# Linear attention woven into an MLP: the second batch's attention rewoven, its neighbour's exps moved ahead, own PSUM banks for one chunk

## The chip, the cores and the metric

The kernel runs on one core of one Trainium2 chip. The metric is the device time of one execution in microseconds (us). All runs quoted gave the reference's result.

## The reference, cut to what matters

```python
def _attn_ref(q, k, v):                 # q, k, v: (8 batches, 8 heads, 576, 64)
    q_s = exp(q - max);  q_s = q_s / sum over the last axis
    k_s = exp(k - max);  k_s = k_s / sum over the sequence
    kv = np.einsum('bhsd,bhse->bhde', k_s, v)
    return np.einsum('bhsd,bhde->bhse', q_s, kv)

def _moe_ref(x, w_in, w_out, beta):     # x: (4608, 512)
    h = x @ w_in                        # (4608, 2048)
    g = h * (1.0 / (1.0 + np.exp(-beta * h)))
    return g @ w_out                    # (4608, 512)
```

## The kernel before: the parts that matter

The rows are handled in nine chunks of 512. Chunk n takes batch n's first 512 rows, one chunk the eight remainders. For each chunk TensorE does 64 products for `h` (16 tiles, four products each) and 64 for the output, `acc`; the scalar engine does a tanh per h tile and VectorE makes `g` from it. The attention of the next batch is woven between those products: exp of q, its sums and division, transposes of q; exp of k, a cast of v, the `kv` products; then `x = kv` times `q`, and casts of x into `xT`.

There are eight PSUM banks (H0 to H2, A0, A1, X0, X1, K), and each h tile is given one by name. A bank can be written again only when its last reader is done; for an h tile the last reader is the VectorE instruction that makes `g`. `LAG = 4` keeps the output products four h tiles behind.

```python
    def h_bank(n, i):
        ...                                   # chunk 0 has its own list
        if n == 1 and i < 7:
            return ("A0", "H0", "H2", "H1", "A1", "K", "X0")[i]
        return f"H{(n * NJ + i + 1) % 3}"
```

Batches 0 and 1 are done early and by hand. Batch 0 is the head of the kernel; batch 1 stands between the output products of chunk 0 (`b_mm(m)` emits m of them) and the first h tiles of chunk 1 (`unit_mm(1, i, k0, k1)`). `eq_exp, eq_sum, eq_div, eq_t` treat q, `ek_exp` k, `ev_cast` v; `ekv_mm` is the kv product with a column of ones that gives the sums, and `eks_mm` computes the sums alone, ahead of it.

```python
    def batch_1():
        b_mm(32)
        eq_exp(1, 0)
        eq_exp(1, 1)
        eq_sum(1, 0)
        eq_div(1, 0, nc.gpsimd)
        b_mm(16)
        ...                                   # k exps, eq_sum(1, 1), eq_div(1, 1, nc.gpsimd), v casts
        b_mm(12)
        eq_t(1, 0, "X0", nc.vector)
        ekv_open(1, 0, ("X1", "K"))
        ekv_mm(1, 0)
        ...                                   # normalise, k exps of half 1, eq_t(1, 1)
        b_mm(2)
        x_group(1, (0,), ["X0", "H1"])
        ...
        b_mm(2)
        ekv_open(1, 1, ("X1", "K"))
        eks_mm(1, 1)
        ...                                   # v casts; unit_mm(1, 0..4, 0, 1)
        ekv_mm(1, 1)
        ...
        x_group(1, (1,), ["X0", "X1"])
        ...
        for m in range(2):
            q_exp(2, m)                       # two of batch 2's four; the others between tanhs
        ...
```

The head, cut to the lines that matter:

```python
    ev_cast(0, 0, 1, nc.gpsimd)               # GpSimd casts the second part of v's first half
    eq_t(0, 0, "X0", nc.scalar)
    dummy(1)                                  # a product that only keeps TensorE at work
    ekv_open(0, 0, ("X1", "K"))
    ekv_mm(0, 0)                              # needs that cast
    ...
    eks_mm(0, 1)
    bt = bank("A1", [P, 4, 4], F32, "bt")
    for i in range(4):
        nc.tensor.transpose(bt[:, i], beta_r[:, i:CH:4], identf[:])
    x_group(0, (0,), ["X0", "A0"])
```

The softmax here doesn't subtract the row's maximum and nothing guards it: scores larger than these inputs give would overflow.

## Time and profile before

| | before |
|---|---|
| time, median of three runs | 287.14 us (286.94 to 287.20) |
| time of the execution that was profiled | 286.0 us, at a mean granted clock of 1.000 |
| span of the profile | 284.3 us |
| first output product of chunk 0 starts | 29.70 us |
| fifth h tile of chunk 1 done | 52.78 us |
| first h product of chunk 2 | 69.40 us |
| products of h and acc | 0.2163 us each, one after another |

The profile's last 215 us are an unbroken row of products, so everything that this change could move lies before 70 us.

### The profile page before, as it was taken

To read this page: it belongs to the slowest core of one execution; us is meant where nothing else is said; L and a number is where in the kernel's file an instruction comes from. 1 tells how busy PE (TensorE), PEld (TensorE's weight loads), DVE (VectorE), ACT (ScalarE), POOL (GpSimd) and SP (SyncE) were. 2 spreads that over 40 slices of the span, in tenths; PEclk is the share of its full clock that TensorE was granted. 3 is DMA by queue.
4 is the path that set the end of the run, shared out by engine and by line. 5 is a ranking of instruction groups with operands and counts; after the bars stand their busy time and mean duration, and the time that the engine had idled before them with its cause. 6 is when DMAs were issued, how large, how long until landed. Compare 5 with 4: busy or idle time off the path is not lost.

```text
span 284.3 us, 4675 instructions
## 1 busy us (share of the span) xinstructions
PE 275.3 (97%) x1708; PEld 136.0 (48%) x1708; DVE 154.7 (54%) x283; ACT 168.2 (59%) x280; POOL 73.1 (26%) x120
## 2 busy tenths in 40 slices
PE   7599999999999999999999999999999999999995
PEld 3455445344454445444444444444444444444444
DVE  2858356886856385647664665467553333344401
ACT  4656374985974578557854785568453544454411
POOL 3378851360451045103610261017000000000000
PEclk9999999999999999999999999999999999999999
DMA  7999999749879916990699149903310200031112
GB/s 234 378 391 408 386 384 357 273 83 362 223 159 323 243 72 141 335 284 0 147 285 324 43 111 292 322 35 90 98 37 2 75 37 37 2 75 37 38 75 74
DMA packets 51559, 51.69 MB, mean 182 GB/s; under 512 B 21068, under 2 KB 41932, under 8 KB 51536
## 3 DMA queue, kind: packets, MB, share of 16 engines
q1 hardware_dynamic: 51360, 51.33, 59.8%
q8 instruction: 13, 0.21, 0.3%
q14 instruction: 10, 0.08, 0.1%
q10 hardware_dynamic: 144, 0.07, 0.1%
q0 software_dynamic: 32, 0.01, 0.0%
HBM read 38.28 MB, written 9.44 MB: 168 GB/s over the span
## 4 chain that ended last, share of the span: by engine, by line
PE 91%; ACT 3%; DMA 3%; DVE 1%; SPq 1%; issue 0%; ACTq 0%
PE acc L511 44%; PE h L459 43%; DMA v<-in_v_dram 3%; PE x L410 2%; PE kv L386 2%; ACT Ek L230 1%; DVE g L473 1%; ACT xT L152 1%; ACT th L471 0%; ACT kvn L281 0%; PE kv L258 0%; SPq L117 0%; ACT qT L152 0%; PE xt L424 0%; DVE qT L166 0%
## 5 line engine op out<-in xcount | busy, mean ns | idle before, releaser
L473 DVE SCALAR_TENSOR_TENSOR g<-th,h 128x512 bf16<-128x512 bf16 x144 | 97.4, 685 | 97.4 <-ACT th L471 97.1
L471 ACT ACTIVATE th<-h,beta_h 128x512 bf16<-128x512 f32 x144 | 97.2, 687 | 84.5 <-PE h L459 82.5
L511 PE MATMUL acc<-w_out_b,g 128*128 128x512 bf16 (+2 forms) x608 | 145.5, 368 | 0.5 <-DVE g L473 0.4
L459 PE MATMUL h<-xT,w_in_b 128*128 128x512 bf16 x512 | 129.1, 379 | 0.6 <-ACT xT L152 0.6
L459 PEld LDWEIGHTS <-w_in_b 128*128 128x128 bf16 x576 | 64.9, 113 | 61.4 <-issue 1.4
L511 PEld LDWEIGHTS <-g 128*128 128x128 bf16 x608 | 56.9, 98 | 65.5 <-issue 3.2
L317 POOL TENSOR_TENSOR Eq<-Eq,qz 128x512 bf16<-128x512 bf16 x24 | 25.1, 1049 | 87.2 <-issue 41.0
L540 ACT ACTIVATE o<-acc 128x512 f32<-128x512 f32 x34 | 20.1, 592 | 10.0 <-PE acc L511 10.0
L161 POOL TENSOR_SCALAR_AFFINE_SELECT va<-v 128x256 bf16<-128x256 f32 (+2 forms) x53 | 20.3, 420 | 8.2 <-DMA v<-in_v_dram 7.9
L357 ACT ACTIVATE Ek<-k 128x640 bf16<-128x640 f32 x24 | 17.5, 729 | 0.0
L315 DVE TENSOR_REDUCE qz<-Eq 128x8 f32<-128x512 bf16 x24 | 16.2, 677 | 0.5 <-ACT Eq L307 0.5
L459 PE MATMUL h<-xTt,w_in_b 128*128 128x512 bf16 x64 | 16.4, 379 | 0.0
L307 ACT ACTIVATE Eq<-q 128x512 bf16<-128x512 f32 x24 | 14.9, 624 | 0.0
L166 DVE CAST xT<-x 128x512 bf16<-128x512 f32 x16 | 10.9, 684 | 0.8 <-PE x L410 0.8
L152 ACT CAST xT<-x 128x512 bf16<-128x512 f32 x16 | 9.3, 579 | 2.2 <-PE x L410 2.2
L161 POOL TENSOR_SCALAR_AFFINE_SELECT w_in_b<-wi 128x512 bf16<-128x512 f32 x16 | 9.5, 612 | 3.0 <-DMA wi<-in_moe_w_in_dram 2.8
L201 DVE TENSOR_REDUCE qz<-Eq 128x16 f32<-128x1024 bf16 x4 | 4.9, 1218 | 9.8 <-ACT Eq L194 9.8
L343 POOL TENSOR_TENSOR Et<-Et,zt 128x512 bf16<-128x512 bf16 x4 | 4.2, 1042 | 21.0 <-DVE zt L342 21.0
L194 ACT ACTIVATE Eq<-q 128x1024 bf16<-128x1024 f32 x4 | 4.2, 1056 | 8.4 <-DMA q<-in_q_dram 8.4
L161 POOL TENSOR_SCALAR_AFFINE_SELECT w_out_b<-wo 128x1024 bf16<-128x1024 f32 x8 | 8.3, 1039 | 1.9 <-DMA wo<-in_moe_w_out_dram 1.8
L584 PE MATMUL warm<-zf 128*128 128x512 f32 (+2 forms) x12 | 7.1, 731 | 1.5 <-DVE zf L551 1.5
L529 DVE TENSOR_SCALAR o<-acc 128x256 f32<-128x256 f32 (+1 forms) x2 | 0.7, 358 | 9.7 <-PE acc L511 9.7
(53 smaller groups left out, 86.8 us busy)
## 6 DMA issues: line engine op xcount, KB each, us to landing
q<-in_q_dram SPq DMA_DIRECT2D x16, 512.0 KB, 5.6
out_dram<-o SPq DMA_DIRECT2D x31, 256.0 KB, 4.2
k<-in_k_dram SPq DMA_DIRECT2D x24, 320.0 KB, 7.1
v<-in_v_dram SPq DMA_DIRECT2D x24, 320.0 KB, 7.5
wo<-in_moe_w_out_dram SPq DMA_DIRECT2D x8, 512.0 KB, 11.0
wi<-in_moe_w_in_dram SPq DMA_DIRECT2D x6, 512.0 KB, 8.2
k<-in_k_dram SPq DMA_DIRECT2D x4, 576.0 KB, 9.0
v<-in_v_dram SPq DMA_DIRECT2D x6, 288.0 KB, 8.6
```

What stands on the lines that cost most here:

```text
L152: nc.scalar.copy(dst, src)
L161: nc.gpsimd.affine_select(out=dst, in_=src, pattern=[[0, n]], base=0, channel_multiplier=0, compare_op=ALU.is_equal, fill=fill0,)
L166: eng.tensor_copy(dst, src)
L307: nc.scalar.activation(by_pair(Eq[b], m).rearrange("p t h d -> p h t d"), ld["q", b, hf][:, a : a + 2, :].rearrange("p h (t d) -> p h t d" ...
L315: nc.vector.tensor_reduce(z, e, axis=AX.X, op=ALU.add)
L317: nc.gpsimd.tensor_tensor(e, e, z.unsqueeze(3).to_broadcast((P, NT, 2, D)), ALU.mult)
L357: nc.scalar.activation(Ek[b][:, :, h0:h1, :].rearrange("p t h d -> p h t d"), ld["k", b, hf][:, a : a + h1 - h0, :].rearrange("p h (t d) - ...
L459: nc.tensor.matmul(hs[n, i][:], w_in_b[:, kt, blk * CH + r : (blk + 1) * CH : 4], rhs_a(n, kt), start=(kt == 0), stop=(kt == KT - 1),)
L471: nc.scalar.activation(th[:], h[:], ACTF.Tanh, scale=beta_h[:, i // 4, i % 4 : i % 4 + 1])
L473: nc.vector.scalar_tensor_tensor(out=g[:], in0=th[:], scalar=1.0, in1=h[:], op0=ALU.add, op1=ALU.mult)
L511: nc.tensor.matmul(acc[n, st][:, c0:c1], gs[n, j][:, min(st, 3) * P : (min(st, 3) + 1) * P], w_out_b[:, j, c0:c1], start=(j == 0), stop=(j ...
L540: nc.scalar.activation(o[:], acc[n, st][:], ACTF.Copy, scale=0.5)
```

## The change

The intent is to take the small waits of TensorE out of batch 1 and chunk 1. The core of the diff:

```diff
     def h_bank(n, i):
-        if n == 1 and i < 7:
-            return ("A0", "H0", "H2", "H1", "A1", "K", "X0")[i]
-        return f"H{(n * NJ + i + 1) % 3}"
+        if n == 1:
+            return ("A0 X1 K X0 A1 H0 H2 H1 X1 H0 H2 H1 H0 H2 H0 H1").split()[i]
+        return f"H{(n * NJ + i) % 3}"
 ... b_mm: one h tile more of lag for chunk 1, j < 4
 ... head:
+    bt = bank("A1", [P, 4, 4], F32, "bt")     # the four beta transposes, before the first of q
 ...
-    dummy(1)
+    dummy(1, 2 * P)
 ...
-    ev_cast(0, 1, 1, nc.scalar, 0, 3)
-    ev_cast(0, 1, 1, nc.vector, 3, 6)
-    ev_cast(0, 1, 1, nc.gpsimd, 6, KT9)
+    ev_cast(0, 1, 1, nc.vector, 0, 5)
+    ev_cast(0, 1, 1, nc.gpsimd, 5, KT9)
     ekv_rk(0, 1)
+    ekv_mm(0, 1)                              # was after the casts of w_in
 ... batch_1:
-        eq_div(1, 0, nc.gpsimd)
-        b_mm(16)
+        eq_div(1, 0, nc.vector)
         for c in range(2):
             ek_exp(1, 0, c)
+        b_mm(20)
         eq_sum(1, 1)
 ...                                           # eq_div(1, 1, nc.vector), k exps earlier
+        b_mm(3)
+        ekv_open(1, 0, ("H0", "H1"))
         ekv_mm(1, 0)
+        b_mm(1)
+        eq_t(1, 1, "H2", None)
 ...
-        eks_mm(1, 1)                          # the pass for the sums alone is gone
 ...
+        b_mm(4)
+        x_group(1, (0,), ["X0", "H0"])
+        ekv_open(1, 1, ("X1", "K"))
+        ekv_mm(1, 1)
 ...
+        b_mm(4)
 ...
+        x_group(1, (1,), ["H1", "H2"])
 ...
-        for m in range(2):
+        for m in range(4):
             q_exp(2, m)                       # batch 2's exps of q, all ahead of chunk 1's tanhs
 ...
-        for m in range(2):
+        for m in range(3):
             q_norm(2, m)
 ... chunks 1 and on:
-            for g in range(2):                # batch 2's x, two groups of four products
-                at(n, 12 + 2 * g, ... x_group(b, (g,), ["X0", "X1"]))
-            at(n, 10, ... x_group(b, (0, 1), ["X0", "X1", "A0", "K"]))
+        at(n, s + 10, ... x_group(b, (0, 1), ["H1" if n == 1 else "A0", "X0", "X1", "K"]))
```

More of the change, by code (lines that the diff above doesn't have):

```diff
@@ L502, in b_mm @@
             n, st, j = bq[pos[0]]
-            if n * NJ + j + LAG > done_a[0] and done_a[0] < NCH * NJ - 1 and n:
+            if n * NJ + j + LAG + (n == 1 and j < 4) > done_a[0] and done_a[0] < NCH * NJ - 1 and n:
                 break
@@ L595 @@
     eq_div(0, 1, nc.vector)
-    nc.vector.tensor_reduce(even[:], evens[:], axis=AX.X, op=ALU.add)
     ev_cast(0, 0, 1, nc.gpsimd)
+    bt = bank("A1", [P, 4, 4], F32, "bt")
+    for i in range(4):
+        nc.tensor.transpose(bt[:, i], beta_r[:, i:CH:4], identf[:])
     eq_t(0, 0, "X0", nc.scalar)
-    dummy(1)
+    dummy(1, 2 * P)
     ekv_open(0, 0, ("X1", "K"))
@@ L607 @@
     ekv_norm(0, 0, nc.vector, nc.scalar)
+    nc.vector.tensor_scalar(
+        beta_h[:], bt[:].rearrange("p i b -> p b i"), 0.5, None, op0=ALU.mult
+    )
+    nc.vector.tensor_reduce(even[:], evens[:], axis=AX.X, op=ALU.add)
     ekv_open(0, 1, ("X1", "K"))
     eks_mm(0, 1)
-    bt = bank("A1", [P, 4, 4], F32, "bt")
-    for i in range(4):
-        nc.tensor.transpose(bt[:, i], beta_r[:, i:CH:4], identf[:])
     x_group(0, (0,), ["X0", "A0"])
     ev_cast(0, 1, 0, nc.gpsimd)
-    ev_cast(0, 1, 1, nc.scalar, 0, 3)
-    ev_cast(0, 1, 1, nc.vector, 3, 6)
-    ev_cast(0, 1, 1, nc.gpsimd, 6, KT9)
+    ev_cast(0, 1, 1, nc.vector, 0, 5)
+    ev_cast(0, 1, 1, nc.gpsimd, 5, KT9)
     ekv_rk(0, 1)
+    ekv_mm(0, 1)
     x_out(0, 0, nc.scalar)
@@ L622 @@
         cast_w_in(0, k0, nc.gpsimd)
-    ekv_mm(0, 1)
     ekv_norm(0, 1, nc.vector, nc.scalar)
-    nc.vector.tensor_scalar(
-        beta_h[:], bt[:].rearrange("p i b -> p b i"), 0.5, None, op0=ALU.mult
-    )
     x_out(0, 1, nc.vector)
@@ L663, in batch_1 @@
         eq_sum(1, 0)
-        eq_div(1, 0, nc.gpsimd)
-        b_mm(16)
+        eq_div(1, 0, nc.vector)
         for c in range(2):
             ek_exp(1, 0, c)
+        b_mm(20)
         eq_sum(1, 1)
-        eq_div(1, 1, nc.gpsimd)
-        ev_cast(1, 0, 0, nc.vector)
-        ev_cast(1, 0, 1, nc.vector, 0, 4)
-        ev_cast(1, 0, 1, nc.scalar, 4, KT9)
-        b_mm(12)
-        eq_t(1, 0, "X0", nc.vector)
-        ekv_open(1, 0, ("X1", "K"))
+        eq_t(1, 0, "X0", None)
+        ev_cast(1, 0, 0, nc.gpsimd)
+        ev_cast(1, 0, 1, nc.scalar, 0, 4)
+        ev_cast(1, 0, 1, nc.gpsimd, 4, KT9)
+        eq_div(1, 1, nc.vector)
+        for c in range(2):
+            ek_exp(1, 1, c)
+        b_mm(3)
+        ekv_open(1, 0, ("H0", "H1"))
         ekv_mm(1, 0)
+        b_mm(1)
+        eq_t(1, 1, "H2", None)
         ekv_rk(1, 0, D)
         ekv_norm(1, 0, nc.vector, nc.scalar)
-        for c in range(2):
-            ek_exp(1, 1, c)
-        eq_t(1, 1, "H2", nc.vector)
-        b_mm(2)
-        x_group(1, (0,), ["X0", "H1"])
-        x_out(1, 0, nc.scalar)
-        x_out(1, 1, nc.vector)
-        b_mm(2)
-        store(0, 3)
-        ekv_open(1, 1, ("X1", "K"))
-        eks_mm(1, 1)
+        eq_out(1, 0, nc.vector)
         ev_cast(1, 1, 0, nc.gpsimd)
-        for i in range(2):
-            unit_mm(1, i, 0, 1)
-        ekv_rk(1, 1)
         ev_cast(1, 1, 1, nc.vector, 0, 3)
@@ L696, in batch_1 @@
         ev_cast(1, 1, 1, nc.gpsimd, 6, KT9)
-        for i in range(2, 5):
+        eq_out(1, 1, nc.vector)
+        b_mm(4)
+        x_group(1, (0,), ["X0", "H0"])
+        ekv_open(1, 1, ("X1", "K"))
+        ekv_mm(1, 1)
+        x_out(1, 0, nc.scalar)
+        ekv_rk(1, 1, D)
+        ekv_norm(1, 1, nc.vector, nc.scalar)
+        x_out(1, 1, nc.vector)
+        b_mm(4)
+        store(0, 3)
+        x_group(1, (1,), ["H1", "H2"])
+        for i in range(4):
             unit_mm(1, i, 0, 1)
-        ekv_mm(1, 1)
-        ekv_norm(1, 1, nc.vector, nc.scalar)
+        x_out(1, 2, nc.scalar)
+        x_out(1, 3, nc.vector)
         for i in range(4):
             unit_mm(1, i, 1, 2)
-        x_group(1, (1,), ["X0", "X1"])
-        x_out(1, 2, nc.scalar)
-        x_out(1, 3, nc.vector)
-        unit_mm(1, 4, 1, 2)
-        for m in range(2):
+        for m in range(4):
             q_exp(2, m)
+        unit_mm(1, 4, 0, 2)
         for i in range(5):
             unit_mm(1, i, 2, 3)
-        for m in range(2):
+        for m in range(3):
             q_norm(2, m)
@@ L725 @@
         for m in range(4):
-            if n == 1 and m < 2:
-                continue
-            i = m if n > 1 else 2 * m - 3
-            at(n, i, lambda b=b, m=m: q_exp(b, m))
-            at(n, i + 1, lambda b=b, m=m: q_norm(b, m))
+            if n == 1 and m > 2:
+                at(n, 4, lambda b=b, m=m: q_norm(b, m))
+            if n > 1:
+                at(n, m, lambda b=b, m=m: q_exp(b, m))
+                at(n, m + 1, lambda b=b, m=m: q_norm(b, m))
         for m in range(4):
@@ L743 @@
         at(n, 9 + s, lambda b=b: kv_group(b))
-        if n == 1:
-            for g in range(2):
-                at(n, 12 + 2 * g, lambda b=b, g=g: x_group(b, (g,), ["X0", "X1"]))
-        else:
-            at(n, 10, lambda b=b: x_group(b, (0, 1), ["X0", "X1", "A0", "K"]))
+        at(
+            n, s + 10,
+            lambda b=b, n=n: x_group(b, (0, 1), ["H1" if n == 1 else "A0", "X0", "X1", "K"]),
+        )
         for kt in range(KT):
             at(
-                n, 12 + kt // 2 * 2 if n == 1 else 10 + kt // 2,
+                n, s + 10 + kt // 2,
                 lambda b=b, kt=kt: x_out(b, kt, nc.scalar if kt % 2 else nc.vector),
```

## The prediction

> **What bounds the kernel now.** I read the page first, for the engine that sets the span, then the chain of waits in order of time for the stretches where that engine does not run at its steady pace, then the timeline of the two such stretches.
>
> ```profile
> PE 275.3 (97%) x1708; PEld 136.0 (48%) x1708; DVE 154.7 (54%) x283; ACT 168.2 (59%) x280; POOL 73.1 (26%) x120
> ...
> PE   7599999999999999999999999999999999999995
> PE 91%; ACT 3%; DMA 3%; DVE 1%; SPq 1%; issue 0%; ACTq 0%
> ```
>
> TensorE (PE) is busy 97% of the 284.3 us span and is 91% of the chain; only the first slices and the last show it below nine tenths. From about 70 us on, the chain is an unbroken row of "0.86 PE h x4" and "0.86 PE acc x4": 0.865 us for four products of 128x512, so 0.216 us each. The change touches nothing in that steady part except which bank a tile gets. So all that can move lies before 70 us: the head (to 16 us) and batch 1 with chunk 1 (42 to 70 us). The windows of PE say how little idle time they show:
>
> ```profile
> 29.70:42.65 12.95, 12.95 (x61) 1.00 1.06 384
> 42.65:52.78 10.13, 9.22 (x104) 1.00 1.08 362
> 52.78:69.40 16.62, 16.07 (x113) 1.00 0.66 203
> 69.40:75.40 6.00, 6.00 (x29) 1.00 1.13 320
> ```
>
> The second number is busy time. In the middle windows 0.9 and 0.6 us are idle, but a matmul's record (0.38 us) is longer than its 0.216 us step, so a record covers part of a gap. The gaps are better seen from starts:
>
> ```profile
> 46.15 0.38 PE L258 MATMUL kv<-va,Ek 64*128 64x2 bf16 x18 [0.34 <-ACT Ek L230]
> 46.76 1.24 PE L459 MATMUL h<-xT,w_in_b 128*128 128x512 bf16 x5 [0.23 <-ACT xT L152]
> ...
> 50.62 3.18 PE L459 MATMUL h<-xT,w_in_b 128*128 128x512 bf16 x14 [0.34 <-ACT xT L152]
> ...
> 54.24 0.39 PE L511 MATMUL acc<-w_out_b,g 128*128 128x512 bf16 x1 [0.21 <-DVE g L473]
> ...
> 57.30 0.81 PE L511 MATMUL acc<-w_out_b,g 128*128 128x512 bf16 x3 [0.20 <-DVE g L473]
> ```
>
> Each bracket is PE waiting for a small link of batch 1 (exp of k, a cast of x) or for g. Two more rows tell when batch 1 can begin at all, and who does its division:
>
> ```profile
> 36.23 1.06 ACT L194 ACTIVATE Eq<-q 128x1024 bf16<-128x1024 f32 x1 [5.20 <-DMA q<-in_q_dram]
> 38.98 3.84 POOL L205 TENSOR_TENSOR Eq<-Eq,qz 128x1024 bf16<-128x1024 bf16 x2 [3.14 <-DVE qz L202]
> ```
>
> The scalar engine waits 5.2 us for q of batch 1 while the DMA moves about 390 GB/s: batch 1 is anchored to the loads, whatever the head does.
>
> **What the Trainium skill says.** "Perfetto Trace Analysis", section "Identifying the Most-Contended Engine": matmul busy share is not a good measure of nearness to the limit, since matmuls are pipelined. The trace agrees: 0.38 us records at a 0.216 us step, and busy 6.00 of 6.00 where the work is packed, but also 16.07 of 16.62 where, as I count below, 1.3 us is lost. "TensorE: Matmul & The Clock Gate", section "Back-to-back issue gap", gives N/2.4 + 2.5 ns (216 ns for N=512) for an isolated product and about 131 ns sustained; here the sustained step is 216 ns, so the first agrees and the second does not, and I use the measured one. "PSUM — Partial Sum Buffer", section "PSUM bank collisions raise a hardware error", has two engines kept off one bank by semaphores: so a new tile in a bank waits for the last reader. The trace shows it in the head: the first small kv products wait 0.34 us for the scalar engine's kvn, which reads that bank. "SBUF — State Buffer", section "SBUF: two separate sides", has one port pair shared by VectorE and GpSimd, locked for a whole instruction. The head agrees: the division takes 1.23 us on VectorE alone and 1.61 us where a GpSimd cast (9.83 to 10.50 us) overlaps it.
>
> **The change part by part.**
>
> *What it removes.* The separate sums pass of batch 1 (18 products of 64x2): 46.15 to 46.50, 0.35 us of PE, plus its 0.5 us wait. Nothing else of PE's work goes away.
>
> *PE's budget.* From 29.70 us (first output product) to the end of the first five h tiles of chunk 1 PE must do 64 acc and 20 h products, 84 x 0.2163 = 18.2; two groups of transposes of 0.55 (1.1); two kv groups of 0.62 (1.24); two x groups of 0.34 (0.7): 21.2 us. It took 29.70 to 52.78 = 23.1, so 1.9 us are lost (0.35 of it the sums). From there to the first h of chunk 2 it must do 44 h and 20 acc (13.8), kv of batch 2 (0.75) and x (0.7): 15.3, and took 52.78 to 69.40 = 16.6; 1.3 lost. In all 3.2 us of room.
>
> *Head.* The four beta transposes (0.57 us, 13.49 to 14.06 in the chain) sit before x; they move ahead of the first transposes, where PE idles (beta has landed at 1.3 + 4.7 = 6.0; PE is free 7.5 to 8.6). x of batch 0 then starts at about 13.5, its kv at 13.9 and the second x group at about 15.2 instead of 15.60. Worth 0.4 to 0.5 us at 16 us. But what it frees comes before the anchor: PE simply reaches batch 1 earlier and waits for it. I count zero to 0.3 of it.
>
> *Batch 1, walked link by link* (the instruction order of the changed kernel on each engine, with durations from this trace). q at 36.23 and 37.66 as before. VectorE: sum 1.22, reciprocal 0.25, division 1.23, and again: 37.32 + 5.5 = about 43.0 with some port blocking. Before, GpSimd did both in 3.84, to 42.82: the end is the same, but the first half is ready at 40.1 and not 40.9, and GpSimd is free to cast v as it lands. The scalar engine does exp of k (about 39.1 to 40.5, then 42.0 to 43.3; k of the second half I estimate to land at 42 from 32.6 plus 9). kv at about 42.2, one acc, transposes of half 1 at 43.1 (PE waits for the division, perhaps 0.3), four acc to 44.6. Then kvn, copy of qT (0.69) on VectorE, x at about 44.8 (0.2 of waiting). kv of half 1 to 45.8; four acc cover its normalisation, to 46.7; x at 46.8; then 20 h products, 4.33, whose xT casts (0.58 and 0.69) all finish under earlier products. The fifth h ends at about 51.5 instead of 52.78: **1.3 us** earlier.
>
> *q of batch 2.* All four exps stand ahead of the tanh (47.9 to 50.4 on the scalar engine, 4 x 0.63) and three of the four normalisations as well. Before, two exps fell between tanhs and cost the stretch to 58 us its gaps. tanh and g then run at 0.65 to 0.69 against PE's 1.08 per unit. With h tiles on X1, H0, H2, H1 PE no longer waits for g until about the tenth h, whose bank needs g of tile 5, which comes after the last normalisation (0.85): 0.1. The joined x group (8 products) needs kvn, which stands behind g of tile 11: I see about 0.4 of waiting at 62.6. First h of chunk 2 at about 67.3 instead of 69.40. **Sum 2.0 us** with 0.6 of new waits in chunk 1 and 0.5 in batch 1 still there.
>
> **The rivals.** (1) *No net gain.* The division on VectorE stacks all of batch 1 there: two sums, two divisions, two copies, two normalisations, a cast. If the port lock adds 0.4 per division, or the late copy of qT blocks x, PE loses 1 us more and only 0.5 to 1 is left: 286.3. For it: the 1.61 us division. Against: GpSimd has only 2.1 us of casts then. (2) *All the room is taken:* the head's 0.45 comes through and no wait is left: 3.7 us, 283.4. Against: the q loads, which don't move. (3) *A new wait later:* x of chunks 2 and on begins in A0, a bank that waits for an output copy on the scalar engine. Seven products (1.5 us) lie between and the copy takes 0.59; this should not show; if it did, 0.3 in each of six chunks, 286.9. (4) *The loads are the real limit* and h or acc wait for cast weights after an earlier head: w_in's second block is cast by 18.06, needed at about 18.6, so no.
>
> **Range and chances.** 287.14 - 2.0 = 285.1 us. The walk's links are each uncertain by 0.1 to 0.3, so 0.6 to 3.2 us of gain: 283.9 to 286.5. Over 2% would be 5.7 us, more than the 3.2 (or 3.7) there is; 2% slower would need new waits of 5.7 us in a kernel whose steady part is untouched. Faster 0.02, same 0.96, slower 0.02.
>
> **What would show it.** PE's chain with no sums group; bt's transposes near 8 us; second x group of batch 0 near 15.2; kv of batch 1 near 42.2 and transposes of half 1 near 43.1 waiting for VectorE; the fifth h done near 51.5; first h of chunk 2 near 67.3; from there rows of 0.86 without breaks, the end 2 us earlier. It would be wrong if q of batch 1 landed at another time, if PE waited over 0.5 us at one of the kv or x groups, or if A0 caused gaps in each chunk.

## More of the kernel before

The *granted clock* is the share of TensorE's full clock that it was given: 1.000 is full speed.

The page's clock row, in tenths of full speed per slice of 7.1 us, shows nothing amiss in before:

```profile
PEclk9999999999999999999999999999999999999999
```

## The result, and the profile after

| | before | after |
|---|---|---|
| median, four runs each | 287.17 us (286.94 to 287.38) | 284.03 us (284.02 to 284.06) |
| ratio | | 0.9891, 95% interval 0.9874 to 0.9908 |
| span of the profile | 284.3 us at clock 1.000 | 282.3 us at clock 0.994 |

The ratio is the mean time of one kernel's runs over the mean of the other's from the same rounds, so it isn't quite the ratio of the medians. All outputs are right. The change is 1.1% faster: "the same" by the 2% rule, as foretold, and inside the range. The range ran from 283.9, so 284.03 is at its very edge. The gain is 3.14 us where 2.0 was forecast, and the two spans differ by just 2.0. That mismatch is what most of the experiments are about.

The page after, with busy time by engine, the granted clock by slice, and the shares by engine of the chain of work that ended last, followed back through its waits:

```profile
PE 271.9 (96%) x1662; PEld 136.7 (48%) x1690; DVE 156.7 (55%) x283; ACT 167.9 (59%) x279; POOL 70.9 (25%) x120
...
PEclk9899999999999999999999999999999999999999
...
PE 93%; DMA 3%; issue 1%; SPq 1%; DVE 0%; POOL 0%; ACT 0%; ACTq 0%
```

In the chain the scalar engine's 3% and VectorE's 1% of before are gone: the links of batch 1 no longer hold TensorE. New is the 8 in the clock row, in the slice from 7 to 14 us.

The windows of TensorE after, cut at the same events as the prediction's (start and end, length, busy time, granted clock, DMA share, GB/s):

```profile
30.78:42.00 11.22, 11.17 (x52) 1.00 1.06 382
42.00:52.20 10.20, 10.10 (x91) 1.00 1.08 361
52.20:67.56 15.36, 15.20 (x113) 1.00 0.74 229
```

From the first output product to the fifth h tile TensorE took 52.20 - 30.78 = 21.42 us (23.08 before), from there to chunk 2 it took 15.36 (16.62 before). Together 36.78 instead of 39.70, so 2.9 us of the 3.2 us of room are gone. But the first output product came at 30.78 us and not at 29.70: **1.1 us were lost in the head**, which is why chunk 2 starts only 1.84 us earlier. From chunk 2 to the end nothing changed: 284.3 - 69.40 = 214.9 before, 282.3 - 67.56 = 214.7 after.

Batch 1 in the timeline of TensorE after (start, duration, line, operation, count; a bracket would show a wait):

```profile
43.19 0.69 PE L258 MATMUL kv<-va,Ek 64*128 64x130 bf16 x18
43.81 0.39 PE L511 MATMUL acc<-w_out_b,g 128*128 128x512 bf16 x1
44.03 0.61 PE L217 MATMUL tp<-ident,Eq 128*128 128x128 bf16 x8
44.70 0.81 PE L511 MATMUL acc<-w_out_b,g 128*128 128x512 bf16 x3
45.47 0.41 PE L410 MATMUL x<-qT,kvn 64*64 64x512 bf16 x4
45.86 0.68 PE L258 MATMUL kv<-va,Ek 64*128 64x130 bf16 x18
46.48 1.04 PE L511 MATMUL acc<-w_out_b,g 128*128 128x512 bf16 x4
47.44 0.49 PE L410 MATMUL x<-qT,kvn 64*64 64x512 bf16 x4
47.87 5.37 PE L459 MATMUL h<-xT,w_in_b 128*128 128x512 bf16 x23
```

There is no bracket, no group of sums, and 23 h products stand in one row. The fifth h tile ends 20 products after 47.87, at 47.87 + 20 x 0.2163 = 52.20.

The wait that the prediction had placed before the joined x group is missing: VectorE finished kvn at 62.80 us and x started at 63.32. The scalar engine, which the chain to kvn goes through, had caught up by then: the tanh of tile 11, at 60.84, waited for TensorE. Its pace between the exps of k:

```profile
57.45 0.72 ACT L471 ACTIVATE th<-h,beta_h 128x512 bf16<-128x512 f32 x1
58.02 0.78 ACT L357 ACTIVATE Ek<-k 128x640 bf16<-128x640 f32 x1
58.65 0.73 ACT L471 ACTIVATE th<-h,beta_h 128x512 bf16<-128x512 f32 x1
```

A tanh and an exp of k together take 58.65 - 57.45 = 1.20 us, though their records add up to 0.72 + 0.78 = 1.50: the records overlap. The skill's "Perfetto Trace Analysis", section "Per-instruction lifecycle: what the profiler-reported window actually captures", has the record of such an instruction end with the acknowledgement of its last write. The trace agrees with a record that is longer than the step from start to start; the step is what adds up.

### The head, and two kinds of clock

Where did the 1.1 us in the head come from? The timelines of GpSimd, VectorE and TensorE of before:

```profile
9.83 0.67 POOL L161 TENSOR_SCALAR_AFFINE_SELECT va<-v 128x576 bf16<-128x576 f32 x1 [6.33 <-DMA v<-in_v_dram]
9.97 1.61 DVE L205 TENSOR_TENSOR Eq<-Eq,qz 128x1024 bf16<-128x1024 bf16 x1
10.55 0.69 PE L258 MATMUL kv<-va,Ek 64*128 64x130 bf16 x18 [1.01 <-POOL va L161]
```

After:

```profile
10.66 1.05 POOL L161 TENSOR_SCALAR_AFFINE_SELECT va<-v 128x576 bf16<-128x576 f32 x1 [7.15 <-DMA v<-in_v_dram]
...
11.75 1.16 PE L258 MATMUL kv<-va,Ek 64*128 64x130 bf16 x18 [2.02 <-POOL va L161]
```

In the second profile v landed later: the cast started at 10.66 and not 9.83, took 1.05 us and not 0.67, and kv of batch 0 came 1.2 us later, after an idle time of 2.0 us. Then something else happens. The windows of TensorE after, with the granted clock in the column after the count:

```profile
11.00:12.00 1.00, 0.25 (x6) 0.67 1.07 352
12.00:13.00 1.00, 1.00 (x19) 0.50 0.92 316
...
14.00:15.00 1.00, 1.00 (x22) 0.62 1.06 406
```

From 11.34 to 14.76 us, for 3.4 us, TensorE ran at half its clock, and the records of that stretch are longer: 1.16 us for the 18 kv products that took 0.69. The skill's "TensorE: Matmul & The Clock Gate", section "What's actually happening", describes this: a clock that is halved after an idle window of about 3.4 us and full after a busy one, with windows that run freely and don't start with the kernel. The trace agrees on the size, 3.4 us here and twice that in two runs below (e0, e1). But the window ahead was not idle here: TensorE was busy 1.09 of its 3.42 us. And how it ends stays open: after one halved window with 3.00 us of work the clock was full again here, while in e0 a second one followed a window in which TensorE was busy 3.41 of 3.41 us.

### The profile page after: what moved, and what is told of

It is laid out like the page before. It is cut to its first block, busy times and chain, and to the rows that moved or that the text cites. A ratio compares the mean times of both kernels' runs of the same rounds, so it can differ in the third digit from the quotient of the medians.

```text
span 282.3 us, 4607 instructions
## 1 busy us (share of the span) xinstructions
PE 271.9 (96%) x1662; PEld 136.7 (48%) x1690; DVE 156.7 (55%) x283; ACT 167.9 (59%) x279; POOL 70.9 (25%) x120
## 4 chain that ended last, share of the span: by engine, by line
PE 93%; DMA 3%; issue 1%; SPq 1%; DVE 0%; POOL 0%; ACT 0%; ACTq 0%
PE acc L511 44%; PE h L459 44%; DMA v<-in_v_dram 3%; PE kv L386 2%; PE x L410 2%; PE kv L258 1%; PE tp L217 1%; PE warm L584 0%; POOL va L161 0%; SPq L117 0%; PE xt L424 0%; DVE xT L166 0%; DVE kvn L283 0%; SPq L105 0%; ACT o L534 0%
## 5 line engine op out<-in xcount | busy, mean ns | idle before, releaser
L511 PE MATMUL acc<-w_out_b,g 128*128 128x512 bf16 (+2 forms) x590 | 142.8, 368 | 1.7 <-issue 1.1
L459 PE MATMUL h<-xT,w_in_b 128*128 128x512 bf16 x503 | 127.4, 379 | 0.7 <-DVE xT L166 0.3
L161 POOL TENSOR_SCALAR_AFFINE_SELECT va<-v 128x256 bf16<-128x256 f32 (+3 forms) x55 | 21.8, 435 | 14.5 <-DMA v<-in_v_dram 14.2
L584 PE MATMUL warm<-zf 128*128 128x512 f32 (+1 forms) x12 | 7.0, 723 | 1.5 <-DVE zf L551 1.5
L230 ACT ACTIVATE Ek<-k 128x576 bf16<-128x576 f32 x8 | 5.0, 675 | 2.5 <-DMA k<-in_k_dram 2.4
```

The source lines that it names most:

```text
L161: nc.gpsimd.affine_select(out=dst, in_=src, pattern=[[0, n]], base=0, channel_multiplier=0, compare_op=ALU.is_equal, fill=fill0,)
L459: nc.tensor.matmul(hs[n, i][:], w_in_b[:, kt, blk * CH + r : (blk + 1) * CH : 4], rhs_a(n, kt), start=(kt == 0), stop=(kt == KT - 1),)
L511: nc.tensor.matmul(acc[n, st][:, c0:c1], gs[n, j][:, min(st, 3) * P : (min(st, 3) + 1) * P], w_out_b[:, j, c0:c1], start=(j == 0), stop=(j ...
```

## The experiments

Two theories stood against each other for the surplus of 1.1 us over the forecast. **A:** the new head costs or brings something. **B:** the head before and after is exposed alike to when the loads land, and the timed runs of before contain halved clock that its profile, by chance, does not.

### e0: the kernel before once more; e1: the new head alone; e2: all but the head

e0 has no edit. e1 is the kernel after with before's `batch_1`, banks, lag and hooks; e2 is the reverse:

```diff
 e2, against the kernel after
-    bt = bank("A1", [P, 4, 4], F32, "bt")     # and its transposes: back behind the sums of half 1
-    dummy(1, 2 * P)
+    dummy(1)
-    ev_cast(0, 1, 1, nc.vector, 0, 5)
-    ev_cast(0, 1, 1, nc.gpsimd, 5, KT9)
-    ekv_mm(0, 1)
+    ev_cast(0, 1, 1, nc.scalar, 0, 3)
+    ev_cast(0, 1, 1, nc.vector, 3, 6)
+    ev_cast(0, 1, 1, nc.gpsimd, 6, KT9)
 ...                                           # ekv_mm(0, 1) behind the casts of w_in again
```

> The unchanged kernel of before, profiled again. Theory: its usual run is slower than the one profile shown (286.0 us) because PE's clock is halved for about 3 us in the head in the usual run, as it is in the changed kernel's profile (0.50 from 11.3 to 14.6 us): then this profile shows a mean clock under 1.0, its first output product near 30.8 us instead of 29.70, a span near 285.4. Rival: the clock of before is always full and only the changed head halves it: then this profile shows clock 1.000 and 29.7 again. Time itself 287.1.

> Before with the new head alone. Theory (head gains are absorbed by the q loads, and its clock state is the load's doing): within 0.5 us of before, 286.7 to 287.3. Rival (the new head costs the halved clock by itself): against a before at full clock 1.0 us slower. Third: the head's 0.45 us comes through, 286.7.

> The changed kernel with the old head. Theory: the whole gain is the body's, 3.0 us: 284.1, equal to the changed kernel's 284.03. If the new head matters by 0.45 us: 284.5. If the new head costs the clock: 283.0.

e0 took 287.33 us (286.33 to 289.82), ratio 0.999 (0.9936 to 1.0044) to the runs of before beside it, whose median was 287.78 (285.94 to 289.73). e1 took 287.02 (285.84 to 288.39), ratio 0.9969 (0.9924 to 1.0015). e2 took 284.28 (283.29 to 285.47), ratio 0.988 (0.9835 to 0.9925). So the gain is the body's, and the head's alone is too small to be told from nothing.

More telling than the medians is e0's profile: the kernel before, unchanged, and its head was late too. GpSimd, VectorE and TensorE:

```profile
9.99 1.67 POOL L161 TENSOR_SCALAR_AFFINE_SELECT va<-v 128x576 bf16<-128x576 f32 x1 [6.50 <-DMA v<-in_v_dram]
9.91 1.23 DVE L205 TENSOR_TENSOR Eq<-Eq,qz 128x1024 bf16<-128x1024 bf16 x1
11.71 0.69 PE L258 MATMUL kv<-va,Ek 64*128 64x130 bf16 x18 [2.23 <-POOL va L161]
```

The cast starts 0.16 us later than in the first profile of before, at 9.99 instead of 9.83, which is behind the division and not ahead of it; it then takes 1.67 us and not 0.67, and kv starts 1.16 us later. All 14 profiles split in the same way. Where the cast started at 9.87 or earlier, it took 0.67 us and the division 1.43 to 1.70 (5 profiles). Where it started at 9.99 or later, it ended only at 11.6 to 11.8, and the division took 1.22 or 1.23 (9). This is the shared port of VectorE and GpSimd that the prediction cited, and who takes it first is decided by when v happens to land. I read this off the traces; no run here changed that order on purpose.

And e0 was halved for two windows. TensorE in e0:

```profile
14.00:16.00 2.00, 2.00 (x37) 0.50 1.05 401
...
18.00:20.00 2.00, 1.84 (x9) 0.65 1.05 386
```

Its first output product came at 32.19 us, 2.5 us later than in the first profile, and everything behind followed unchanged: 39.69 us to chunk 2, against 39.70. So theory B holds: the head of before does the same in its own runs. In e2's profile, with the same head, one window was halved; in e1's, with the new head, two.

### Sorting all runs by their mean granted clock

One window of 3.4 us at half speed lowers the mean clock of a 285 us span by 3.4 x 0.5 / 285 = 0.006. The runs do fall into steps of that size. Here are those of before in the experiment rounds with e0's (39 runs), and those of after (10 runs, the official four and e11's six, told below):

| mean clock of the run | before: runs, mean time | after: runs, mean time | gain |
|---|---|---|---|
| 0.998 and up (no window) | 13 runs, 286.24 us | 5 runs, 283.78 us | 2.46 us |
| 0.992 to 0.994 (one) | 9 runs, 287.45 us | 5 runs, 284.14 us | 3.31 us |
| 0.986 to 0.988 (two) | 13 runs, 288.43 us | none | |
| 0.981 (three) | 4 runs, 289.80 us | none | |

For before each halved window costs 1.0 to 1.4 us. For after the table says 0.36, but its two rows come mostly from different rounds: four of the five with a window are the official runs, all five without are e11's. e11's own run with a window took 284.57, 0.8 more than the others, and in e2, the same body behind the old head, two runs with a window took 284.73 and 285.19 against a mean of 283.51 without. So what a halved window costs the new body is open, between 0.4 and 1.5 us. All four official runs of after had one. The clocks of before's official timed runs are not on record: their times (286.94 to 287.38) lie above all 13 runs without a window (up to 286.66) and among those with one (286.97 to 287.78). Sorting is not an experiment, though. The next two runs are.

### e3 and e4: work for TensorE while it waits in the head

```diff
-    dummy(1, 2 * P)          # e3, in the kernel after
+    dummy(4, 2 * P)
-    dummy(1)                 # e4, in the kernel before
+    dummy(4, 2 * P)
```

> The changed kernel with three more dummy products of 128x256 in the 2 us in which PE waits for v of batch 0. Theory (the idle PE lets its clock be halved): the clock stays at 1.0, the first kv group takes 0.7 instead of 1.16, the first h products start about 1 us earlier; but q of batch 1 is at 36.4 in any case, so of that 1 us only 0.3 to 0.6 comes through: 283.5. Rival (all of it comes through since PE was never ahead of q): 282.9. If the clock is halved for another reason: 284.0.

> The kernel of before with its clock lottery taken away: dummies in the head keep PE busy while it waits for v, as in the warm changed kernel (283.27). Theory (the clock in the head is what spreads the runs of before, and its body takes 39.7 us from the first output product to the first h of chunk 2 whatever the head does): clock near 1.0, spread under 1 us, body 39.7, time 286.2, so 2.9 above the warm changed kernel. Rival (a third of the gain measured was the clock's): 285.2, 1.9 above.

The profile of TensorE in e3:

```profile
9.07 1.95 PE L584 MATMUL warm<-zf 128*128 128x256 f32 x8
11.73 0.69 PE L258 MATMUL kv<-va,Ek 64*128 64x130 bf16 x18 [0.72 <-POOL va L161]
```

(A dummy leaves two records, so x8 are four dummies.) The idle time falls from 2.02 to 0.72 us. The loads are as late as ever (kv at 11.73), but the clock was 0.998 or more in all 12 runs of these two kernels, and in all 36 of the later kernels with these dummies (e5 to e10). e4 took 286.22 us (285.77 to 286.57), ratio 0.996 (0.9926 to 0.9994), beside a before of 287.35: the mean of e4, 286.17, is that of before's full-clock runs, 286.24. e3 took 283.27 (283.11 to 283.94), ratio 0.9849 (0.9809 to 0.9889). So the dummies are worth about 1.1 us to before (0.2 to 2.1 by the interval), shown, and some 0.6 to 0.8 to after, where the intervals overlap. They also part the late v from the clock. With v late, the first output product came in the old head at 30.08 us at full clock (e4), 31.38 with one halved window (e2) and 32.19 with two (e0); in the new head at 29.62 (e3), 30.78 and 30.80 (after, e11) and 32.11 (e1). So the clock costs the head 0.8 to 1.3 us a window, and the late v little (29.70 in before, with an early v). With the clock at full speed in both, the change is worth 286.22 - 283.27 = 2.95 us by the medians of different rounds, 2.76 by the means.

The body's own gain can be read from e3's profile, since its first output product came at 29.62 us, nearly where the first profile of before has it (29.70), and both ran at full clock (q of batch 1 came 0.6 us later in e3, at 36.82 us). The fifth h tile ended at 51.82 instead of 52.78, 0.96 us earlier, and chunk 2 began at 67.18 instead of 69.40, 2.22 us earlier. (e4 was at 30.08, 53.15 and 69.77.) And here the prediction's walk can be checked in e3's timeline (the fifth h tile ends 20 products after 47.49):

```profile
42.40 0.69 PE L258 MATMUL kv<-va,Ek 64*128 64x130 bf16 x18 [0.30 <-ACT va L152]
...
43.41 0.62 PE L217 MATMUL tp<-ident,Eq 128*128 128x128 bf16 x8
...
47.49 5.37 PE L459 MATMUL h<-xT,w_in_b 128*128 128x512 bf16 x23
...
67.18 1.03 PE L459 MATMUL h<-xT,w_in_b 128*128 128x512 bf16 x4
```

All further kernels are edits of e3, so that the clock stays out. They ran in other rounds and on other chips than e3; before's full-clock runs beside them agree to 0.3 us (means 286.25, 286.02 and 286.28), so differences above that can be read.

### e5: the old weave of batch 1, the rest new

e5 is e3 with before's `batch_1`, except that q of batch 2 stays ahead, and with banks for chunk 1 that fit it:

```diff
-            return ("A0 X1 K X0 A1 H0 H2 H1 X1 H0 H2 H1 H0 H2 H0 H1").split()[i]
+            return ("A0 H0 H2 H1 A1 K X0 X1 H1 H0 H2 H1 H0 H2 H0 H1").split()[i]
-        eq_div(1, 0, nc.vector)
+        eq_div(1, 0, nc.gpsimd)
 ...                                           # the old order, with eks_mm(1, 1)
```

> The warm changed kernel with the old weave of batch 1 (sums pass, division on GpSimd, casts and kv inside chunk 1's h tiles), but all four q exps ahead and own banks kept. Theory (the weave is worth what batch 1 lost, at most 1.9 us, less 0.8 that the warm kernel gives back to the q loads): 284.5, 1.2 above the warm changed kernel, all of it lost before the fifth h ends. Rival (what counts is the chunk 1 part): 283.5.

285.16 us (284.57 to 285.30), ratio 0.9923: 1.9 us above e3, where 1.2 was expected, all before the fifth h tile. The fifth h tile ended at 51.98 in an early head, that is 23.07 us after the first output product, before's value (23.08). With the new weave this stretch takes 22.20 us in e3 and 21.42 after a late head, in after. Chunk 1 took 16.07 and not 15.36, with this at its start:

```profile
53.57 0.39 PE L511 MATMUL acc<-w_out_b,g 128*128 128x512 bf16 x1 [0.57 <-DVE g L473]
```

So in the profiles 0.87 us are lost before the fifth h tile and 0.71 behind it. With the old weave the q exps end at 51.98 and their norms on VectorE at 52.96 (50.40 and 51.45 in e3), and the first g stands behind them. The parts help each other.

### e6: the q exps not ahead

```diff
-        for m in range(4):
+        for m in range(2):
             q_exp(2, m)
-        for m in range(3):
+        for m in range(2):
             q_norm(2, m)
+                at(n, 2 * m - 3, lambda b=b, m=m: q_exp(b, m))     # m = 2, 3, as before
+                at(n, 2 * m - 2, lambda b=b, m=m: q_norm(b, m))
```

> The warm changed kernel with only two q exps of batch 2 ahead of chunk 1 and two between its tanhs, as before. Theory (those two exps late on the scalar engine cost chunk 1 its gaps): 0.6 to 1.0 us above the warm changed kernel, 284.0, with waits for g at the second to fourth output product. Rival (own banks are what removes the gaps): 283.4.

284.57 us (284.11 to 285.40), ratio 0.9907: 1.3 us above e3. The wait came, but once and at the tenth h tile, whose bank H0 needs the g of the sixth, rather than among the first output products:

```profile
57.97 1.02 PE L459 MATMUL h<-xT,w_in_b 128*128 128x512 bf16 x4 [0.58 <-DVE g L473]
```

### e7: the old banks from the sixth h tile on

```diff
-        if n == 1:
+        if n == 1 and i < 5:
             return ("A0 X1 K X0 A1 H0 H2 H1 X1 H0 H2 H1 H0 H2 H0 H1").split()[i]
 ...                                           # and batch 2's x in two groups on X0, X1 again
```

> The warm changed kernel with three banks in turn for the h tiles of chunk 1 from the sixth on, and x of batch 2 in two halves on X0 and X1, as before. Theory (banks matter little once tanh is on time): 0.2 to 0.4 us above the warm changed kernel, 283.6. Rival (h tiles wait for g of three tiles before): 1 us above, 284.3.

285.05 us (284.86 to 285.60), ratio 0.9925: 1.8 us above e3, where I had expected a few tenths. TensorE:

```profile
55.93 1.02 PE L459 MATMUL h<-xT,w_in_b 128*128 128x512 bf16 x4 [1.36 <-DVE g L473]
```

and VectorE ahead of it:

```profile
54.41 0.68 DVE L315 TENSOR_REDUCE qz<-Eq 128x8 f32<-128x512 bf16 x1
...
55.24 1.83 DVE L473 SCALAR_TENSOR_TENSOR g<-th,h 128x512 bf16<-128x512 bf16 x3
```

With three banks in turn, the ninth h tile needs the g of the sixth, and this one stands behind the last sum of q on VectorE. With its own banks the ninth takes X1, last read by the g of the second tile, which is done. The prediction's sum had no part for the banks at all, and this wait is 1.36 us: the banks are what lets the q norms stand ahead. (The edit also splits batch 2's x again; the trace shows no wait there.)

### e8: the divisions back on GpSimd

```diff
-        eq_div(1, 0, nc.vector)
+        eq_div(1, 0, nc.gpsimd)
-        eq_div(1, 1, nc.vector)
+        eq_div(1, 1, nc.gpsimd)
```

> The warm changed kernel with batch 1's two divisions on GpSimd again (1.94 us each there against 1.23). Theory: the second half's transposes wait for the second division, and v's casts queue behind it on GpSimd, so batch 1 ends 0.5 to 1.0 us later: 283.9. Rival (the weave hides it): 283.3.

284.02 us (283.85 to 284.42), ratio 0.9875: 0.75 above e3. Both groups of transposes waited for GpSimd, as expected, the first 0.94 us and the second, at 44.04, 0.69:

```profile
41.15 0.62 PE L217 MATMUL tp<-ident,Eq 128*128 128x128 bf16 x8 [0.94 <-POOL Eq L205]
...
44.04 0.62 PE L217 MATMUL tp<-ident,Eq 128*128 128x128 bf16 x8 [0.69 <-POOL Eq L205]
```

### e9, e10: the first q of batch 1 loaded earlier

e9 issues the load of batch 1's first half of q before the last two rows of `w_out`. e10 also moves one cast of v up on the scalar engine:

```diff
     for j0 in range(0, NJ, 2):
+        if j0 == 14:
+            load_q(1, 0)
         load_w_out(j0)
 ...
+        ev_cast(1, 0, 1, nc.scalar, 0, 4)     # e10 alone: before b_mm(20), not behind it
         b_mm(20)
```

> The warm changed kernel with the first q load of batch 1 issued ahead of the last w_out load. Theory (with a warm head, batch 1 is anchored to its loads): exp of q starts at about 35.1 instead of 36.4, the transposes of half 1 no longer wait for the division, but the first kv group still waits for the scalar engine's cast of v at about 42: 0.2 to 0.4 us faster than 283.27, so 283.0. Rival (the q load is no anchor): 283.3.

> The last one, with the scalar engine's cast of batch 1's v ahead of the first two output copies. Theory: the cast is done at about 41.3, kv starts when PE reaches it (about 41.6), batch 1 ends 0.5 to 0.8 us earlier than in the warm changed kernel: 282.6. Rival (v and k land too late for it): 283.0.

e9 took 283.34 us (282.97 to 284.78), e10 283.45 (283.29 to 283.81); ratios 0.986 and 0.9855. Neither is to be told from e3's 283.27, so the expected 283.0 and 282.6 were not met. e9's profile has the exp of q at 34.79 us instead of 36.82 in e3, but the second half of q still came at 37.59 (38.32 in e3), and its first h of chunk 2 at 66.45 comes from a run whose v also landed early. These two runs don't settle whether more is to be had there.

### e11: the kernel after once more

> The changed kernel unchanged, timed over more rounds beside the one before. Theory: its runs spread by about 1 us with the clock of the head (less than the 3.8 of before, as late PE arrivals are partly absorbed by the wait for loads that an early PE has anyway), median near 284.1; the profile shows from the first output product to the first h of chunk 2 36.8 us where PE came late and up to 37.6 where it came early. Rival: always 284.03.

283.84 us (283.44 to 284.57), ratio 0.987 (0.9824 to 0.9916). Five of its six runs were at full clock, the profiled one was not. It took 37.26 us from the first output product to chunk 2, where 36.8 was expected for a late head. In that profile the predicted wait at the joined x group did appear, for another reason than the predicted one: the transposing DMA of q was late.

```profile
63.82 0.63 PE L410 MATMUL x<-qT,kvn 64*64 64x512 bf16 x8 [0.41 <-DMA qT<-Eq]
```

That DMA was issued at 57.6 us in both profiles of after; it landed 4.8 us later in the official one and 6.2 us later here. e2 shows the same wait of 0.43, again behind 6.2 us; the other 12 profiles have 4.4 to 5.4 us and no such wait.

**The best version** is e3, the changed kernel with four dummies: 283.27 us, ahead of before by 1.5%. It is below after's two medians (284.03 and 283.84), but not by more than their intervals leave open.

## Why the prediction was right, and which terms were off

The range and the mechanism held: TensorE's small waits in batch 1 and chunk 1 were the room, and in the official profile nothing took their place. The number is in part luck: a surplus of 1.1 us, from a clock that the prediction doesn't mention, just fitted into a range that was made for other reasons. Point by point:

- **Batch 1, predicted 1.3 us.** From a like start (before and e3) it is 0.96, from the late start in after 23.08 - 21.42 = 1.66. The walk itself holds to 0.3 us: in e3 kv came at 42.40 (42.2 predicted), transposes at 43.41 (43.1), x at 44.83 (44.8), the second x at 47.07 (46.8), the fifth h at 51.82 (51.5). VectorE's two sums and divisions ended at 43.36 us, in after at 42.93 (43.0 predicted). e8 confirms the division's move from the other side: undone, it costs 0.75.
- **Chunk 1, predicted 0.7 to 0.8 us** (2.0 less 1.3; 16.6 less 15.8) with 0.5 of new waits in it (the sum says 0.6, its parts make 0.5). Mis-sized: the stretch was 15.36 us and not the 15.8 from 51.5 to 67.3, a gain of 1.26. "The joined x group (8 products) needs kvn, which stands behind g of tile 11: I see about 0.4 of waiting at 62.6" is the term that fell: kvn was done 0.5 us before x started. Adding up record durations (1.50 us per pair of tanh and exp, at a pace of 1.20) would give such a lag.
- **Banks.** The sum gave them no term of their own, only a remark. e7 shows 1.8 us hanging on them. The weave, the q exps and the banks, undone one at a time (1.9, 1.3 and 1.8), add up to 5.0 us where all bring 2.95: in each of the three traces the new wait is one for g.
- **The head, predicted zero to 0.3.** With the new body it is zero: e2's three full-clock runs have a mean of 283.51 us and after's five of 283.78, which is no gain, though at full clock and with v late the new head brought the first output product 0.46 us earlier (e3 against e4), about what was counted for it at 16 us. In the profile after, the second x group of batch 0 came at 16.75 and not near 15.2, with v late and the clock halved. The beta transposes did move ahead, to 6.62.
- **"But what it frees comes before the anchor."** Half right. q of batch 1 did come at the same time whatever the head did (its exp at 36.23 to 36.83 us in before, e0, e1, e3, e4 and after). But in before's body TensorE didn't depend on it: every difference of the head went through whole (39.69 or 39.70 us to chunk 2 in each of four profiles). In the new body an early start is partly lost: to the fifth h tile it is 22.20 us in e3 and 21.42 in after, e11 and e2, which start later. But e11 and e2 lost 0.41 and 0.43 again to the late transposing DMA. So heads that were 1.16, 1.18 and 1.76 us later than e3's left chunk 2 0.38 (after), 0.88 (e11) and 1.47 us (e2) later.
- **The starting value** is the step that failed most. I subtracted a gain read from a profile at full clock (286.0 us) from a median (287.14) whose runs, by their times, had mostly a halved window. The two terms above make 2.2 from a like start. Runs at full clock gain 2.46, runs with one halved window 3.31 (table above), and the official ones (3.14) fit the latter: in them after lost less to its late head than before did to its own. That this holds in general is not shown: e11 and e2 lost more.
- **The rivals.** (1), no net gain, is false: 21.42 us from first output product to fifth h. (2), all the room, was nearly right for the body: 36.78 us of the ideal 36.5. It was wrong for the head, which gave nothing. (3), gaps from x in A0, is false: 214.9 and 214.7 us from chunk 2 to the end. (4) is false for the weights, as foretold: after's trace has no wait of TensorE for a cast of them from 15 to 72 us.

## What to carry to other kernels

Before a gain read from a profile is taken off a measured time, compare the profiled run's own time and clock with those of the timed runs: here 1.1 us of 3.1 hid in that difference. When TensorE must wait in the head, give it something to do: four small products kept its clock up in all 48 runs that had them. And undo the parts of a change one by one before crediting any of them, since banks that look like bookkeeping may be what lets another part work at all.

## What the Trainium skill lacked or had wrong

- "TensorE: Matmul & The Clock Gate": its section "Back-to-back issue gap" gives some 131 ns for products of N=512 in a sustained row. Here they stood at 216 ns in the row from 70 us on, which is what the page has for back-to-back products elsewhere.
- The same page has the clock fall after an idle window. It lacks how much work is still too little. Here TensorE was busy 0.88 to 1.56 us of the 3.4 us ahead of a halving (after, e0, e1, e2, e11). Where before's windows began isn't known: of any 3.4 us ending between 9.9 and 13.4 it was busy 1.2 to 2.4, and the clock stayed full. Nor is it clear when the clock comes back: after one window with 3.00 us of work in after, but not after 3.41 of 3.41 us in e0.
- "SBUF — State Buffer": its lock of the port pair, which the first to start gets, is seen. What it lacks is how much the order decides here: a cast starting 0.16 us later took 1.67 us and not 0.67, and kv came 1.16 us later.
- "Perfetto Trace Analysis": it says what a record spans, and that its last part overlaps with the next instruction, but gives no example of records added up. Here a tanh and an exp recorded 0.72 and 0.78 us ran at 1.20 per pair.
- "DMA: Bandwidth & Descriptors": lacks how much the landing of a transposing DMA spreads. Here batch 2's took 4.4 to 5.4 us in 12 profiles and 6.2 in two, and those two cost TensorE 0.41 and 0.43.
